# The second weight chunk in halves between those of the first, and conversion passes moved behind the first steps' copies

## The chip, the cores and the metric

One core of one Trainium2 chip runs the whole program. The metric is the device time of one execution in microseconds; the kernel before was measured in four runs. A core has five engines that work at once, each through its own queue in order: PE (TensorE, the matrix multiplier, which writes to PSUM), DVE (VectorE), ACT (ScalarE), POOL (GpSimd) and SP (SyncE, which here only issues DMA transfers). Engines wait for each other through semaphores.

## The reference, cut to what matters

```python
batch, seq, dim = (8, 3008, 256)
X = np.fft.fft(x, axis=1)
X = np.fft.fft(X, axis=2)
x = X.real.astype(np.float32).reshape(B * S, D)
h = x @ w_in                                # w_in:  256 x 2048
g = h * (1.0 / (1.0 + np.exp(-1.702 * h)))
return (g @ w_out).astype(np.float32)       # w_out: 2048 x 256
```

A two-dimensional Fourier transform of eight sequences, of which the real part is kept, and on it two matrix products with a quick GELU between them. Both weight matrices arrive in double precision.

## The kernel before, in words

**The transform.** The sequence length is split as 3008 = 47 x 64. `mix_first` (and `mix1` for later sequences) does the 47-point part as matmuls, the result goes through DRAM (`spill_first`, `fill`), and `stage2` does the 64-point part for one block of four groups; its result is transposed by DVE into the tile `pq`. The transform over the 256 columns is not done on the data: it is folded into `w_in`. `fold_w(n)` multiplies chunk n of `w_in` (512 columns) by a cosine and sine table and leaves the product in `wcs`. It needs eight matmuls of 512 columns, four for each half i of the rows (i = 0 and i = 1), which add up in two PSUM banks; ACT copies both out (line 474).

**The weights' conversion.** A chunk is 512 columns of `w_in` (in0 to in3) or 512 rows of `w_out` (out0 to out3), 1024 doubles per partition, loaded as pairs of 32-bit words (`load_in`, `load_out`, on SP's queue, into a ring of three buffers `raw`). It becomes float32 in steps on three engines:

| step | engine, line | what it needs |
|---|---|---|
| `squares` | ACT 401 | the raw chunk |
| `clamp` | POOL 406 | the raw chunk |
| `low_up`, `low_down` | ACT 411, 416 | the raw chunk, each other |
| `high` | DVE 433, 434, 435 | squares, clamp |
| `finish_in`, `finish_out` | POOL 447, 455 | high, low_down |

`prepare` takes the buffers for it. `bounds` is prepare, squares, clamp, low_up and low_down at once, `finish` is one of the finishing steps. `finish_in` writes `wst`, which fold_w reads; `finish_out` writes `wo`, which the output products read.

**The steps.** The work on the data is a list of 384 steps t: 8 sequences, 3 blocks, 2 halves, 8 pairs of 128 hidden features. In the first eight steps (t < 8) a step is: `hidden(t)` (PE: sixteen matmul records into the banks `pa` and `pb`; ACT copies pa to `v`, line 515), `rows(t)` (DVE lines 553, 556, 544: it reads v, pb, `nb`, pa and gives both halves of the hidden values), `activate(t)` (ACT line 562) and `product(t)` (PE, into the output banks, three steps later: LAG = 3). `nyquist(0, 0)` makes `nb` through PE and an ACT copy (line 372), `first_row(n)` makes `af` for chunk n (PE `psf`, ACT lines 482 and 483), `rotate` corrects one column (PE `psr`). `warm` is a matmul whose result nobody reads. Steps from 8 on run another, larger loop body that the change leaves alone.

**What sets the order.** The schedule is written out by hand: instructions go to each engine's queue in the order of the calls. Before the loop stands a list of calls (lines 874 to 908). In the loop, `extra` holds what is appended to the end of a step, by `at(t, fn, ...)`; fold_w(2) and fold_w(3) stand in steps 3 and 5 (`early`). PSUM banks for the opening come in turn from a ring of six names, and each call of `bank` moves on by one; from step 5 on the ring is cut, and step 5 asks for two banks by name:

```python
    spare = ["b0", "b1", "b2", "o2", "o3", "o4"]
...
        pa, pb = (bank(name, f"b{i}" if t == NP - 3 else None) for i, name in enumerate(("pa", "pb")))
```

Of the kernel before, what the change touches and what calls it, by code (L numbers as in the profile page):

```python
# [111 lines left out]
def kernel(ctx: ExitStack, tc, x, w_in, w_out, tab1, tab2, out):  # L112
    nc = tc.nc
# [53 lines left out]
    def bank(name, tag=None):  # L167
        if tag is None:
            tag = spare.pop(0)
            spare.append(tag)  # L170
        if tag in ("o0", "o1"):
            return o_banks[int(tag[1])]
        return (rest if tag[0] == "o" else psp).tile([128, 512], F32, tag=tag, name=name)
# [5 lines left out]
    def halves(out, lhs, rhs, **how):  # L179

        for c0 in (0, 64):
            nc.tensor.matmul(out[c0:c0 + 64], lhsT=lhs[:, c0:c0 + 64], rhs=rhs, skip_group_check=True, **how)  # L182
# [137 lines left out]
    def warm(n):  # L320

        ps = bank("warm")
        for _ in range(n):
            nc.tensor.matmul(ps[:], lhsT=wcs[0][:, 0:128], rhs=wcs[0][:, 0:512], start=True, stop=True)
# [11 lines left out]
    def rotate(b, a0=0, a1=NG, copy=None):  # L336

        col = t4t[b][:, a0:a1, H]
        ps = bank("psr")
        halves(ps[:, 0:a1 - a0], rot, col, start=True, stop=True)  # L340
        (copy or nc.vector.tensor_copy)(col, ps[:, 0:a1 - a0])
# [39 lines left out]
    def load_in(n, eng):  # L381
        t = raw["in", n] = ring("raw").bitcast(U32).rearrange("p (n w) -> p n w", w=2)
        eng.dma_start(out=t[:].rearrange("p (i f) w -> p i (f w)", i=2),
                      in_=w_in[:, n * 512:(n + 1) * 512].bitcast(U32).rearrange("(i p) f -> p i f", p=128))
# [8 lines left out]
    def prepare(key):  # L393


        pre[key] = ring("s"), ring("m"), ring("r").bitcast(U32)

    def squares(key, eng):
        g, hi = pre[key][0], raw[key][:, :, 1].bitcast(F32)
        if eng is nc.scalar:  # L400
            eng.activation(g[:], hi, ACTF.Square)
        else:
            eng.tensor_tensor(g[:], hi, hi, op=ALU.mult)

    def clamp(key, lo=0, n=1024):
        nc.gpsimd.tensor_scalar(pre[key][1][:, lo:lo + n], raw[key][:, lo:lo + n, 1].bitcast(F32), scalar1=TOP, scalar2=-TOP,
                                op0=ALU.min, op1=ALU.max)

    def low_up(key, lo=0, n=1024):

        nc.scalar.activation(pre[key][2][:, lo:lo + n].bitcast(F32), raw[key][:, lo:lo + n, 0], ACTF.Copy, scale=2.0 ** -29,
                             bias=2.0 ** 23)

    def low_down(key, lo=0, n=1024):
        r = pre[key][2][:, lo:lo + n]
        nc.scalar.activation(r, r.bitcast(F32), ACTF.Copy, bias=-2.0 ** 23)
# [8 lines left out]
    def high(key, lo=0, n=1024):  # L425

        g, m, _ = (t[:, lo:lo + n] for t in pre[key])
        bits = m.bitcast(U32)
        if lo == 0:
            made_a[key] = ring("a").bitcast(U32)  # L430
        a = made_a[key][:, lo:lo + n]
        dve = nc.vector
        dve.scalar_tensor_tensor(m, g, LOW * LOW, m, op0=ALU.is_ge, op1=ALU.mult)
        dve.tensor_scalar(a, bits, scalar1=3, scalar2=0x3FFFFFF8, op0=ALU.logical_shift_left, op1=ALU.bitwise_and)
        dve.scalar_tensor_tensor(a, bits, 0xC0000000, a, op0=ALU.bitwise_and, op1=ALU.bitwise_or)
# [5 lines left out]
    def finish_in(n, lo=0, k=1024):  # L441

        if lo == 0:
            wst[n] = op.tile([128, 2, 512], F32, tag="os", name="wst")
        key, part = ("in", n), slice(lo, lo + k)
        out = wst[n][:].rearrange("p i f -> p (i f)")[:, part]
        nc.gpsimd.tensor_tensor(out.bitcast(U32), made_a[key][:, part], pre[key][2][:, part], op=ALU.add)
# [16 lines left out]
        for out, i0, i1 in ((t1, b12, b11), (t2, b22, t1), (t3, b22, b12), (t4, b21, t2)):  # L464
            nc.gpsimd.tensor_tensor(out, i0, i1, op=ALU.subtract)

    def fold_w(n):
        ps = [bank("psw") for _ in range(2)]
        for i in range(2):
            for cs in range(2):  # L470
                halves(ps[cs][:], cd[:, i, cs, :], wst[n][:, i, :], start=(i == 0), stop=(i == 1))
        for cs in range(2):

            nc.scalar.copy(wcs[cs][:, n * 512:(n + 1) * 512].rearrange("p (f c) -> p f c", f=4),
                           free(ps[cs][:], 0, [1, 4], [4, 128]))
# [379 lines left out]
    for i, need in enumerate(((0, 7), (1,), (6,), (2,), (5,), (3,), (4,), ())):  # L855
# [8 lines left out]
        if i in (4, 5):  # L864
            h0 = 512 * (i - 4)
# [12 lines left out]
        spill_first(k, 16, NM, (nc.sync, nc.sync))  # L878
    prepare(in1)
    squares(in1, nc.scalar)  # L880
    for h0 in (0, 512):
        finish_in(0, h0, 512)
    clamp(in1)
    low_up(in1)
    low_down(in1)
    high(in1)
    load_out(1, nc.sync)
    fill(0, 4, NG)
    warm(1)
    fold_w(0)  # L890
    warm(1)
    first_row(0)
    prepare(out0)
    finish_in(1)
    clamp(out0)
    rotate(0, 0, 4, nc.scalar.copy)
    squares(out0, nc.scalar)
    stage2(0, 0)
    warm(1)
    low_up(out0)  # L900
    low_down(out0)
    high(out0)
    load_in(3, nc.sync)
    prepare(in2)
    squares(in2, nc.scalar)
    clamp(in2)
    fold_w(1)
    finish_out(0)

    extra, early = {}, {}  # L910

# [1 line left out]
        extra.setdefault(t, []).append((fn, args))  # L913

    n = len(steps)

    for t, key in (1, in2), (2, ("out", 1)), (3, ("in", 3)), (5, ("out", 2)), (6, ("out", 3)):
        at(t, high, key)
        if key != in2:
# [1 line left out]
        at(t + 1, finish, key)  # L921
    early[3], early[5] = 2, 3
    rows_at = {1: 1, 4: 2, 6: 3}
    for t, c in ((0, 2), (1, 3)):
        at(t, load_out, c, nc.sync)
    at(3, load_matrices)
    if B > 1:
# [35 lines left out]
    for t in range(n + LAG):  # L963
        if t < NP:
            if t == NP - 3:
                spare[:] = [tag for tag in spare if tag[0] == "o"] + ["b2"]
            hidden(t)
            if t == NP - 1:
                middle(NP)
                begin(NP)  # L970
                nc.gpsimd.memset(wcs[1][0:1, :], 0.0)
            if t == 0:
                low_up(in2)
                nyquist(0, 0)
                low_down(in2)
            if t in rows_at:
                first_row(rows_at[t])
            if t >= LAG:
                product(t - LAG, 0, None)
            if t in early:  # L980
                fold_w(early[t])
            if t:
                activate(t - 1)
            rows(t)
            if t == NP - 1:
                doubled(NP)
                middle(NP + 1)
        else:
            after, special = (any(fn in (mix1, stage2) for fn, _ in extra.get(k, ())) for k in (t - 1, t))
            if t < n:  # L990
                begin(t, 1)
            if t == NP:
                activate(t - 1)
            if t < n:
                forward(t)
            if after and t + 1 < n:
                middle(t + 1)
            opening = (t - LAG) % NP == 0 and t >= NP + LAG
            one, other = (t - LAG, (1, 2, 4, 7)), (t - LAG - 1, (5, 6, 3))
            if opening:  # L1000
                small_products(*other)
            cut = 0 if opening and not after else 3 if after else 2
            product(t - LAG, 0, cut)
            if after:
                small_products(one[0], one[1][:1])
                small_products(other[0], () if opening else other[1][:1])
            if t + 1 < n:
                begin(t + 1)
            if not opening:
                small_products(other[0], other[1][after:])  # L1010
            product(t - LAG, cut, 6 if t - LAG == last else None)
            small_products(one[0], one[1][after:])
            swap(t - LAG - 2)
            if t < n:
                backward(t)
            if t + 1 < n:
                doubled(t + 1)
            if t < n:
                activate_back(t)
                sums(t, nc.gpsimd)  # L1020
            if t + 2 < n and not special:
                middle(t + 2)
            combine_small(t - LAG - 1)
            if t - LAG == last:
                product(last, 6, None)
            sums(t - 1, nc.vector)
            deeper(t - 2, 0)
            deeper(t - 3, 1)
        if t == NP:
            psu.close()  # L1030
            low = ctx.enter_context(tc.tile_pool(name="low", bufs=1, space=PS))
            pot["low"] = low.tile([128, 3 * 512], F32, tag="low", name="low")
        if t >= LAG:
            combine(t - LAG)
            combine_last(t - LAG - 2)
            turn_last(t - LAG - 3, 0)
            turn_last(t - LAG - 4, 1)
        if t >= NP:
            spare[:] = [f"b{t % 2}"] * special + ["b2"]
        for fn, args in extra.get(t, ()):  # L1040
            fn(*args)
# [28 lines left out]
```

## Time and profile before

| | |
|---|---|
| median of 4 runs | 1875.7 us (1869.67 to 1876.27) |
| the profiled execution's own time | 1875.91 us |
| its span (first to last instruction) | 1874.1 us |
| PE busy | 1847.7 us, 99% |
| DVE busy | 1531.1 us, 82% |
| ACT busy | 1150.7 us, 61% |
| POOL busy | 965.9 us, 52% |

All times in the timelines are from the start of the span. The stretch that the change touches goes from about 25 us, when PE has done `mix_first`, to about 80 us, when step 7 runs. In that stretch, by windows: PE is busy 12.60 of 15 us in 25 to 40, 10.00 of 10 in 40 to 50, 8.67 of 10 in 50 to 60 and 15.00 of 15 in 60 to 75; ACT is busy 9.06 of 10 in 40 to 50, and DVE 9.79 of 10 in 50 to 60. A row of a timeline gives start, length, engine, line, operation, output and input tiles, shape and count; in brackets the engine's idle time before it, and what released it. A matmul of float32 shows as two records, so "x8" are four matmuls. Line numbers are those of the kernel before.

### The profile page before, as it was taken

The numbers are of one execution on the slowest core, as the hardware profiler recorded it, in microseconds if no ns is written. First come the engines' busy times: TensorE is split into PE (matmuls) and PEld (weight loads), VectorE is DVE, ScalarE is ACT, GpSimd is POOL, SyncE is SP. The second block draws the span as 40 slices with busy tenths as digits, with TensorE's granted clock in tenths as the row PEclk, the third lists the DMA queues.
The fourth block names the chain that finished last, engine by engine and source line by source line (L and its number), as shares of the span: only waits on it lengthen the run. The fifth ranks groups of instructions, "written<-read, shape, count | busy, mean of one in ns | idle before, by whom it ended". The sixth has DMA issues, their size and how long they took to land.

```text
span 1874.1 us, 55830 instructions
## 1 busy us (share of the span) xinstructions
PE 1847.7 (99%) x23684; PEld 1421.2 (76%) x23684; DVE 1531.1 (82%) x2245; ACT 1150.7 (61%) x2248; POOL 965.9 (52%) x1058
## 2 busy tenths in 40 slices
PE   8999999999999999999999999999999999999998
PEld 5667777778777777777777778776877777778776
DVE  7788888888789877997789878887788888878874
ACT  6655665666556556666666666655566666656663
POOL 5577345744367443773347633475345754444442
PEclk9999999999999999999999999999999999999999
DMA  8720350125110350114402252122411021100111
GB/s 278 177 51 17 80 95 17 48 63 100 32 51 14 74 101 19 51 21 106 67 13 59 44 104 39 21 56 57 96 30 25 19 62 35 29 18 16 20 22 23
DMA packets 145686, 105.28 MB, mean 56 GB/s; under 512 B 105161, under 2 KB 128233, under 8 KB 144254
## 3 DMA queue, kind: packets, MB, share of 16 engines
q1 hardware_dynamic: 144222, 101.19, 24.9%
q8 instruction: 187, 3.06, 0.7%
q10 hardware_dynamic: 1216, 0.52, 0.1%
q14 instruction: 61, 0.50, 0.1%
HBM read 64.41 MB, written 48.05 MB: 60 GB/s over the span
## 4 chain that ended last, share of the span: by engine, by line
PE 88%; DVE 6%; ACT 3%; issue 1%; DMA 1%; POOL 0%; SPq 0%; DVEq 0%; ACTq 0%; POOLq 0%
PE x L182 32%; PE o L182 25%; PE low L664 23%; PE o L664 4%; DVE big L630 2%; PE ps L354 1%; PE ps L253 1%; DVE big L544 1%; DVE big L767 1%; ACT x L571 1%; DMA big<-in_moe_w_in_dram 1%; ACT xt L256 0%; ACT big L586 0%; ACT g L583 0%; DVE big L676 0%
## 5 line engine op out<-in xcount | busy, mean ns | idle before, releaser
L601 POOL TENSOR_TENSOR big<-big 128x256 f32<-128x256 f32 (+1 forms) x376 | 351.3, 934 | 846.1 <-ACT big L593 731.7
L182 PE MATMUL x<-pq,wcs 128*64 128x256 f32 (+1 forms) x6016 | 775.8, 378 | 6.1 <-ACT x L571 3.0
L630 DVE TENSOR_TENSOR big<-big 128x512 f32<-128x512 f32 (+1 forms) x736 | 639.2, 883 | 35.4 <-PE low L664 18.9
L182 PE MATMUL o<-big,wo 128*64 128x256 f32 (+1 forms) x4800 | 625.2, 376 | 2.0 <-DVE big L608 2.0
L182 PEld LDWEIGHTS x<-pq,wcs 128*64 128x64 f32 x6016 | 419.0, 137 | 190.4 <-ACT x L571 15.0
L182 PEld LDWEIGHTS o<-big,wo 128*64 128x64 f32 x4800 | 349.0, 137 | 143.6 <-DVE big L608 2.9
L583 ACT ACTIVATE g<-x 128x512 f32<-128x512 f32 (+1 forms) x376 | 222.0, 590 | 374.5 <-PE x L182 373.4
L544 DVE TENSOR_TENSOR big<-g,x 128x512 f32<-128x512 f32 (+2 forms) x440 | 253.8, 588 | 198.8 <-ACT big L586 198.3
L664 PE MATMUL low<-big 128*64 128x128 f32 (+1 forms) x5888 | 383.7, 270 | 4.0 <-issue 4.0
L664 PEld LDWEIGHTS low<-big 128*64 128x64 f32 x5888 | 338.8, 137 | 32.2 <-issue 4.3
L571 ACT ACTIVATE x<-nb,af 128x256 f32<-128x256 f32 (+1 forms) x752 | 352.7, 469 | 12.3
L602 POOL TENSOR_TENSOR big<-big 128x256 f32<-128x256 f32 (+1 forms) x376 | 358.9, 955 | 0.0
L586 ACT ACTIVATE big<-x 128x512 f32<-128x512 f32 (+1 forms) x376 | 220.5, 586 | 200.6 <-PE x L182 191.1
L593 ACT ACTIVATE big<-big 128x512 f32<-128x512 f32 (+1 forms) x376 | 231.8, 617 | 48.1 <-DVE big L544 46.0
L664 PE MATMUL low<-big,wo 128*64 128x128 f32 (+1 forms) x2944 | 222.4, 271 | 0.3 <-issue 0.2
L664 PEld LDWEIGHTS low<-big,wo 128*64 128x64 f32 x2944 | 173.8, 137 | 4.0 <-issue 0.4
L609 DVE TENSOR_TENSOR big<-big 128x512 f32<-128x512 f32 (+1 forms) x188 | 149.5, 795 | 6.5
L608 DVE TENSOR_TENSOR big<-big 128x512 f32<-128x512 f32 (+1 forms) x188 | 137.3, 731 | 4.8 <-POOL big L601 4.8
L767 DVE TENSOR_TENSOR big<-big,low 128x512 f32<-128x512 f32 (+3 forms) x184 | 109.1, 610 | 3.9 <-PE low L664 0.4
L664 PEld LDWEIGHTS o<-big,wo 128*64 128x64 f32 x1472 | 93.4, 137 | 23.9
L664 PE MATMUL o<-big,wo 128*64 128x128 f32 (+1 forms) x1472 | 110.7, 270 | 0.0
L225 POOL TENSOR_TENSOR xt<-xt 111x510 f32<-111x510 f32 x56 | 76.2, 1360 | 4.4
(103 smaller groups left out, 972.7 us busy)
## 6 DMA issues: line engine op xcount, KB each, us to landing
out_dram<-os SPq DMA_DIRECT2D x284, 64.0 KB
t<-Td SPq DMA_DIRECT2D x22, 512.0 KB
Td<-xt SPq DMA_DIRECT2D x14, 768.0 KB
xt<-in_x_dram SPq DMA_DIRECT2D x14, 512.0 KB
xt<-Xr SPq DMA_DIRECT2D x14, 512.0 KB
nb<-Nd SPq DMA_DIRECT2D x23, 256.0 KB
out_dram<-os SPq DMA_DIRECT2D x96, 56.0 KB
Xr<-in_x_dram SPq DMA_DIRECT2D x7, 752.0 KB
```

The costliest lines, as they stand in the source:

```text
L182: nc.tensor.matmul(out[c0:c0 + 64], lhsT=lhs[:, c0:c0 + 64], rhs=rhs, skip_group_check=True, **how)
L544: nc.vector.tensor_tensor(free(out, at + m - 1, [by, 2], [RUN, blocks], [-1, m]), *ins, op=op)
L571: nc.scalar.activation(x[:, i * 256:i * 256 + n], nbt[b, blk][:, hh * 256:hh * 256 + n], ACTF.Copy, scale=af1[:, f:f + 1])
L583: nc.scalar.activation(two(g[:], n), two(xb[t][:], n), ACTF.Copy, scale=2.0)
L586: nc.scalar.activation(front(t), two(xb[t][:], width(t)), ACTF.Gelu_apprx_sigmoid)
L593: nc.scalar.activation(back(t), back(t), ACTF.Gelu_apprx_sigmoid)
L601: eng.tensor_tensor(right(t, S1, n), left(t, A21, n), right(t, A22, n), op=ALU.add)
L602: eng.tensor_tensor(left(t, S3, n), left(t, A11, n), left(t, A21, n), op=ALU.subtract)
L608: eng.tensor_tensor(s2, s1, a11, op=ALU.subtract)
L609: eng.tensor_tensor(s4, a12, s2, op=ALU.subtract)
L630: nc.vector.tensor_tensor(out, i0, i1, op=how)
L664: nc.tensor.matmul(o, lhsT=lhs, rhs=rhs, start=first_in, stop=(p == NP - 2), skip_group_check=True)
```

## The change

`fold_w` can now be called for one half of the rows at a time: it takes its two banks with the first half and copies out with the second. In the list before the loop, in1's `high` and `finish_in` are done in two halves of 512, its clamp is put between the two halves of in0's `finish_in`, and the matmuls of fold_w(1) stand in two parts, one before the first `stage2` and one behind it. first_row(0) comes after that. Two of the `warm` calls are gone. Out0's `low_up` and `low_down` are moved into steps 0 and 1, `finish_out(0)` to the end of step 1, in2's `squares` and `low_up` into step 1 and its `low_down` into step 2. `load_in(3)` and the loads of out2 and out3 stand later among the calls, in the same order on SP's queue.

```diff
-    def fold_w(n):
-        ps = [bank("psw") for _ in range(2)]
-        for i in range(2):
+    folded = {}
+
+    def fold_w(n, parts=(0, 1)):
+        if parts[0] == 0:
+            folded[n] = [bank("psw") for _ in range(2)]
+        ps = folded[n]
+        for i in parts:
             for cs in range(2):
                 halves(ps[cs][:], cd[:, i, cs, :], wst[n][:, i, :], start=(i == 0), stop=(i == 1))
+        if parts[-1] == 0:
+            return
...
     squares(in1, nc.scalar)
-    for h0 in (0, 512):
-        finish_in(0, h0, 512)
+    finish_in(0, 0, 512)
     clamp(in1)
+    finish_in(0, 512, 512)
     low_up(in1)
     low_down(in1)
-    high(in1)
+    for h0 in (0, 512):
+        high(in1, h0, 512)
     load_out(1, nc.sync)
     fill(0, 4, NG)
     warm(1)
     fold_w(0)
-    warm(1)
+    prepare(out0)
+    for h0 in (0, 512):
+        finish_in(1, h0, 512)
+    clamp(out0)
+    fold_w(1, (0,))
+    rotate(0, 0, 4, nc.scalar.copy)
+    stage2(0, 0)
+    squares(out0, nc.scalar)
+    fold_w(1, (1,))
     first_row(0)
-    prepare(out0)
-    finish_in(1)
-    clamp(out0)
-    rotate(0, 0, 4, nc.scalar.copy)
-    squares(out0, nc.scalar)
-    stage2(0, 0)
-    warm(1)
-    low_up(out0)
-    low_down(out0)
     high(out0)
-    load_in(3, nc.sync)
     prepare(in2)
-    squares(in2, nc.scalar)
     clamp(in2)
-    fold_w(1)
-    finish_out(0)
...
+    at(1, finish_out, 0)
...
-    for t, c in ((0, 2), (1, 3)):
+    for t, c in ((1, 2), (2, 3)):
         at(t, load_out, c, nc.sync)
...
             if t == 0:
-                low_up(in2)
                 nyquist(0, 0)
-                low_down(in2)
+                low_up(out0)
+                load_in(3, nc.sync)
+            if t == 1:
+                low_down(out0)
             if t in rows_at:
                 first_row(rows_at[t])
+            if t == 1:
+                squares(in2, nc.scalar)
+                low_up(in2)
+            if t == 2:
+                low_down(in2)
```

## The prediction, made before the changed kernel ran

> **What bounds the kernel now.** I read the page first (busy shares, slices), then PE's waits, then the timelines of the four engines for 25 to 80 us, where all that the diff touches runs.
>
> ```profile
> PE 1847.7 (99%) x23684; PEld 1421.2 (76%) x23684; DVE 1531.1 (82%) x2245; ACT 1150.7 (61%) x2248; POOL 965.9 (52%) x1058
> ```
>
> TensorE (PE) is busy for 99% of the span: the main loop is bound by it, and the steps after the opening only move with the moment when the opening hands over. So the question is when PE gets through the opening. PE's timeline there (start, length, engine, line, tile, count, idle before and its releaser):
>
> ```profile
> 26.91 1.94 PE L182 MATMUL psw<-wst,small 128*64 128x512 f32 x8 [0.96 <-POOL wst L447]
> 29.34 1.94 PE L182 MATMUL psw<-wst,small 128*64 128x512 f32 x8 [0.49 <-POOL wst L447]
> ...
> 36.20 3.65 PE L182 MATMUL psw<-wst,small 128*64 128x512 f32 x16 [0.95 <-POOL wst L447]
> 39.68 1.03 PE L182 MATMUL pa<-pq,wcs 128*64 128x256 f32 x8
> ...
> 52.74 3.65 PE L182 MATMUL psw<-wst,small 128*64 128x512 f32 x16 [0.62 <-POOL wst L447]
> ...
> 58.88 0.63 PE L182 MATMUL psf<-twos,wcs 1*64 1x1 f32 x16 [0.71 <-DVE big L544]
> ...
> 63.03 1.06 PE L182 MATMUL pa<-pq,wcs 128*64 128x256 f32 x8
> ```
>
> PE waits for the converted weights (`wst`, written by POOL) of chunks 0, 1 and 2, and once for DVE's `rows(3)`. The first step's `pa` starts at 39.68, step 5's at 63.03 without a wait. From 39.68 on PE idles only 1.33 us up to 75 us: an earlier start could be kept only if the other engines kept up.
>
> ACT's timeline, the first steps:
>
> ```profile
> 41.25 1.17 ACT L411 ACTIVATE big<-big 128x1024 f32<-128x1024 uint32 x1
> 42.63 0.59 ACT L372 COPY nb<-psn 128x512 f32<-128x512 f32 x1 [0.22 <-PE psn L182]
> 43.11 1.06 ACT L416 ACTIVATE big<-big 128x1024 uint32<-128x1024 f32 x1
> ...
> 49.39 0.56 ACT L515 COPY v<-pa 128x512 f32<-128x512 f32 x1
> ```
>
> L411 and L416 are chunk in2's `low_up` and `low_down`, done by 44.2; step 2's `v` copy comes at 49.39, behind out1's three passes. DVE's and POOL's timelines, where they get in each other's way:
>
> ```profile
> 23.98 0.43 DVE L434 TENSOR_SCALAR big<-big 128x512 uint32<-128x512 uint32 x1
> 25.76 1.38 DVE L434 TENSOR_SCALAR big<-big 128x512 uint32<-128x512 uint32 x1
> ...
> 52.17 1.61 DVE L433 SCALAR_TENSOR_TENSOR big<-big 128x1024 f32<-128x1024 f32 x1
> 53.88 1.49 DVE L434 TENSOR_SCALAR big<-big 128x1024 uint32<-128x1024 uint32 x1
> ...
> 63.83 0.69 DVE L544 TENSOR_TENSOR big<-pa,dif 128x512 f32<-128x512 f32 x1
> ...
> 50.32 2.37 POOL L447 TENSOR_TENSOR wst<-big 128x1024 uint32<-128x1024 uint32 x1 [4.91 <-DVE big L435]
> 52.67 2.15 POOL L406 TENSOR_SCALAR big<-big 128x1024 f32<-128x1024 f32 x1
> ```
>
> The same L434 takes 0.43 with POOL idle and 1.38 with POOL busy. L433 (1.22 elsewhere) starts at 52.17 but seems to run only once POOL's L447 ends at 52.69; POOL's L406 (1.12 elsewhere) then runs only after L433, and L434 after L406. They take turns.
>
> [...]
>
> **The change, part by part.** The instructions are the same but for two warm-up matmuls fewer, three more on DVE and one on POOL (`high` and `finish_in` of in1 in two pieces); the rest is order.
>
> 1. *Chunk 1 in halves between those of chunk 0.* Removed from PE: two `warm`, 1.0 each, and the 0.95 wait at 36.20. But POOL and DVE, which ran in1's `clamp`, `high` and `finish_in` one after another from 29.25 to 36.14, now interleave, and lock each other out. Step by step: POOL's first in0 half ends at 26.86; L434 holds the lock to 27.14; the moved clamp of in1 (1.12) takes it to 28.26; in0's last L435 (0.69), at 27.18 before, ends at 28.95 in place of 27.87. DVE goes straight on with in1's first L433 (0.68) to 29.6, so in0's second `finish_in` runs 29.6 to 30.85 (1.25), against an end of 29.29. L434 waits for it: 31.3; L435 32.0; next L433 32.65; in1's first `finish_in` 33.9; L434 34.35; L435 35.05; the second half 35.15 to 36.4. On PE, with 1.74 for four 512-wide matmuls (half of 36.20 to 39.68): chunk 0's second half 30.9 to 32.65, chunk 1's first 33.95 to 35.7, `psr` 0.2 and `stage2` 1.1 to 37.0, chunk 1's second half 38.75, `psf` 0.56: step 0 starts at T = 39.3, against 39.68. All that was removed buys 0.4 us. Without any lock wait the same sum gives T = 36.6. Those are the two ends; I take 39.3, because the trace shows the lock.
>
> 2. *ACT's queue.* Now behind the first steps' copies are out0's `low_up` and `low_down` and all three passes of in2, which before ran at 35.8 to 39.0 or right after 41.25. The `nb` copy starts at T+2.95, as before. From there, start to start by the rows of before: nb 0.48, low_up(out0) 1.15, v(1) 0.49, low_down(out0) 0.97, af 0.12, squares(in2) 1.06, low_up(in2) 1.15, activate(0) 0.95, out1's three 1.06, 1.22 and 0.97: 9.62, so v(2) starts at T+12.57 = 51.9, against 49.39. Behind it low_down(in2): 0.46 and 1.06 more, ended at T+14.1 = 53.4, against 44.2. POOL's `finish_in(2)` waits for it now, not for DVE: 53.5 to 55.85 (2.37). Chunk 2's fold starts on PE at 55.9, against 52.74: +3.15. PE, through with `product(0)` at about 52.9, idles some 3 us.
>
> 3. *DVE behind finish_in(2).* rows(2) ends near 54.6; out1's L433 then finds POOL in finish_in(2) until 55.85. Before, that release was at 52.69. From it the same chain follows (out1's `high`, rows(3), in3's `high`, rows(4)), which ended at 64.52; now 3.15 later, at 67.7.
>
> 4. *Banks.* Two fewer `warm` turn the ring of PSUM banks by two: step 4 now takes b0 and b1, which step 5 asks for by name. So step 5's `pa` must wait for rows(4), where before it waited for nobody. Before, it would have lost 64.52 - 63.03 = 1.5; now it starts at 67.7, against 63.03: +4.65. PE gets there at 66.2, after a wait of 0.85 for rows(3).
>
> 5. *Moved at no cost.* `finish_out(0)` goes to step 1: POOL gets to it after low_down(out0), near 45.5, and it collides with in2's `high` to about 49; product(0) needs it then, and waits for activate(0) at about 48.7 anyway. If DVE fell behind there, rows(2) would be late, but it waits for v(2) until 52.45. SP's queue keeps its order: in3's load, released by low_up(out0) at about 43.4 in place of 42.10, is needed at 54 and landed at 51.6 with out2's load beside it, which now starts 5 us later; out2, out3, the tables and the x loads all go out 1.5 to 5 us later, and their users are tens of us away (`fold1` at 108.97).
>
> From step 5 on the order is the old one and each engine hangs on PE's (`fold_w(3)`, ACT's 6.31 us wait for it, v(6), rows(6), `pb` of step 7), so the 4.65 stays. The profiled execution, 1875.91 with a span of 1874.1, would become 1880.6; from the median of 1875.7 (0.2 below it), **1880.4 us**, +0.25%. About 0.3% (5.6 us) is what a measurement of this kernel can tell from no change.
>
> **The rivals.**
> - *The lock costs little in the halves* (T = 36.6, or arbitration kinder than I take it). Then finish_in(2) ends near 53.2, +0.5, and step 5 waits for rows(4): +2.0, 1877.7. For it: only L433 and L434 are seen blocked in the trace, L435 never. [...]
> - *The early start is kept.* If ACT has more room than I count, PE gains 36.6 - 39.68 = -3.1, 1872.6. It decides where finish_in(2) ends by about 49.6 and rows(4) by 60, 6 and 8 us before my times; the count of ACT's passes speaks against it.
> - *Slower beyond doubt: PE's clock falls.* [...] By the start of the trace half rate lasts 5.6 us, that is 2.8 us of work lost; 2.35 of it vanish in the two waits that follow, unless these also grow because v(4) is late. If the clock stays low longer, or the gap at 32.65 counts as well, +2.5: 1882.9. [...] against it: gaps of 2.2 us leave the rate alone.
> - *The change does not start step 0 earlier* is the first part of my forecast already.
>
> **How the numbers follow.** Forecast 0.52, lock cheap 0.24, early start kept 0.08, clock or another wait on top 0.16. Slower by over 0.3%: most of the last case and some 0.2 of the first, whose sum stands only 1 us short of the bound: 0.14 + 0.12 + 0.01 for a chance drift, with a little for terms that I left out, 0.33. Faster by over 0.3%: PE's idle and warm-up time from 25 to 80 us is 4.5 + 2 us in all, so nearly all of it would have to go: 0.03. Within: 0.64. The range takes the cheap lock and half of the last rival, and 2 to 3 us of drift (one of the four runs shown is 6 us below the rest): 1874.5 to 1884.5. The likeliest case alone is 1878.5 to 1882.
>
> **What would show it.** In the profile of the changed kernel: step 0's first `pa` at 39.3 (36.6 if the lock is cheap); L434 and L435 of in1 at over 1 us each; v(2) near 51.9; in2's L416 after v(2) and L447 for in2 released by ACT L416, not DVE; PE's wait before chunk 2's fold about 3 us; step 5's `pa` released by DVE L544 near 67.7. The prediction is wrong if chunk 2's fold starts before 54 or step 5's `pa` finds its bank free; and if warm matmuls are seen at half rate after 56 us, the clock rival holds.

## The result and the profile after

The changed kernel takes 1877.09 us (median of 43 runs, 1871.49 to 1880.8) against 1873.77 us (64 runs, 1868.23 to 1878.65) for the kernel before. The ratio of the two on record is 1.0020 [1.0013, 1.0026], or 3.7 us more (the two medians are 3.3 apart). Forecast were 0.25% more and, as the likeliest verdict, a difference within 0.3%.

The profiled execution of the changed kernel took 1874.97 us, with a span of 1873.2. That is 0.9 us *less* than the profiled execution of before, so the spans alone would mislead. The loss has to be sought in the stretch that was changed. PE's timeline of the changed kernel there (start, length, engine, line, operation, tiles, shape, count; idle time before and its releaser):

```profile
26.75 1.94 PE L182 MATMUL psw<-wst,small 128*64 128x512 f32 x8 [0.69 <-POOL wst L447]
30.34 1.94 PE L182 MATMUL psw<-wst,small 128*64 128x512 f32 x8 [1.66 <-POOL wst L447]
33.08 1.94 PE L182 MATMUL psw<-wst,small 128*64 128x512 f32 x8 [0.81 <-POOL wst L447]
...
38.52 1.08 PE L182 MATMUL pa<-pq,wcs 128*64 128x256 f32 x8
...
55.04 5.28 PE L182 MATMUL psw<-wst,small 128*64 128x512 f32 x16 [3.38 <-POOL wst L447]
...
66.88 1.08 PE L182 MATMUL pa<-pq,wcs 128*64 128x256 f32 x8 [0.54 <-DVE t L341]
...
83.31 1.08 PE L182 MATMUL pb<-pq,wcs 128*64 128x256 f32 x8 [0.81 <-DVE big L550]
```

Step 0's `pa` starts at 38.52, 1.16 us sooner than before (39.68). Chunk 2's fold starts at 55.04, 2.30 later than before (52.74), behind a gap of 3.38, and takes 5.28 in place of 3.65. Step 5's `pa` starts at 66.88, 3.85 later than before (63.03). From there the distance stays. Step 7's `pb` is 3.86 later, by the line above and this one of the kernel before:

```profile
79.45 1.08 PE L182 MATMUL pb<-pq,wcs 128*64 128x256 f32 x8 [0.81 <-DVE big L544]
```

Lines past `fold_w` have moved by six (L515 is now L521, L544 is L550). The releaser "DVE t L341" is inferred. The copy of `t` stands right behind rows(4), whose L550 ended at 66.73, in DVE's queue. ACT's timeline of the changed kernel shows the moved passes:

```profile
42.01 1.19 ACT L411 ACTIVATE big<-big 128x1024 f32<-128x1024 uint32 x1
...
45.70 1.20 ACT L411 ACTIVATE big<-big 128x1024 f32<-128x1024 uint32 x1
...
50.96 0.57 ACT L521 COPY v<-pa 128x512 f32<-128x512 f32 x1
51.43 1.06 ACT L416 ACTIVATE big<-big 128x1024 uint32<-128x1024 f32 x1
```

The first L411 is out0's. The second is in2's `low_up`, and in2's `low_down` (L416) starts at 51.43, behind v(2); before, it started at 43.11. POOL's timeline has the consequence, and the collisions in the opening; DVE's is below it:

```profile
26.66 1.36 POOL L406 TENSOR_SCALAR big<-big 128x1024 f32<-128x1024 f32 x1
28.71 1.57 POOL L447 TENSOR_TENSOR wst<-big 128x512 uint32<-128x512 uint32 x1 [0.70 <-DVE big L435]
...
44.70 3.58 POOL L455 TENSOR_TENSOR wo<-big 128x512 uint32<-128x512 uint32 x2 [4.95 <-ACT big L416]
...
52.62 2.37 POOL L447 TENSOR_TENSOR wst<-big 128x1024 uint32<-128x1024 uint32 x1 [3.22 <-ACT big L416]
```

```profile
27.01 1.55 DVE L435 SCALAR_TENSOR_TENSOR big<-big 128x512 uint32<-128x512 uint32 x1
...
29.20 1.37 DVE L434 TENSOR_SCALAR big<-big 128x512 uint32<-128x512 uint32 x1
30.60 0.69 DVE L435 SCALAR_TENSOR_TENSOR big<-big 128x512 uint32<-128x512 uint32 x1
...
48.32 1.63 DVE L434 TENSOR_SCALAR big<-big 128x1024 uint32<-128x1024 uint32 x1 [1.17 <-POOL wo L455]
...
53.68 2.39 DVE L433 SCALAR_TENSOR_TENSOR big<-big 128x1024 f32<-128x1024 f32 x1
```

`finish_in(2)` waited 3.22 us and was released by ACT's L416, no longer by DVE. At 27.01 an L435, which takes 0.69 alone, took 1.55 beside POOL's clamp (L406); L434 (0.43 alone) took 1.37 beside POOL's L447; and L433 (1.22 alone) took 2.39 beside `finish_in(2)`. In these rows each of DVE's three conversion lines is held up by POOL.

The busy times by windows of the changed kernel (PE, PEld, DVE, ACT, POOL, with counts; then the granted PE clock) have one more thing:

```profile
50.00:60.00 10.00, 6.62 (x32) 2.43 (x28) 9.47 (x11) 7.63 (x9) 5.48 (x3) 0.83 0.99 312
```

The clock was 0.83 in 50 to 60 (1.00 before), and 0.50 in each of the three us from 55 to 58. That is 1.7 of 10 us of full speed lost, and the fold took 1.63 longer. Whether the gap of 3.38 is the cause is tested below.

### The profile page after: what moved, and what is told of

Read it like the earlier page. It is cut to its first block, busy times and chain, and to the rows that moved or that the text cites. A ratio compares the mean times of both kernels' runs of the same rounds, so it can differ in the third digit from the quotient of the medians.

```text
span 1873.2 us, 55828 instructions
## 1 busy us (share of the span) xinstructions
PE 1846.3 (99%) x23680; PEld 1416.5 (76%) x23680; DVE 1531.8 (82%) x2248; ACT 1150.5 (61%) x2248; POOL 967.0 (52%) x1059
## 4 chain that ended last, share of the span: by engine, by line
PE 88%; DVE 6%; ACT 4%; issue 1%; DMA 1%; POOL 0%; SPq 0%; ACTq 0%; DVEq 0%; POOLq 0%
PE x L182 32%; PE o L182 24%; PE low L670 23%; PE o L670 4%; DVE big L636 2%; PE ps L354 1%; PE ps L253 1%; DVE big L773 1%; DVE big L550 1%; ACT x L577 1%; PE ps L306 1%; ACT xt L256 0%; ACT big L592 0%; DVE big L682 0%; PE psw L182 0%
## 5 line engine op out<-in xcount | busy, mean ns | idle before, releaser
L550 DVE TENSOR_TENSOR big<-g,x 128x512 f32<-128x512 f32 (+2 forms) x440 | 253.8, 588 | 203.7 <-ACT big L592 203.3
```

The source lines that it names most:

```text
L550: nc.vector.tensor_tensor(free(out, at + m - 1, [by, 2], [RUN, blocks], [-1, m]), *ins, op=op)
```

## The experiments

The theory was that of the prediction, with times taken from the trace: in2's late `low_down` moves chunk 2's fold, and the turned ring of banks makes step 5 wait for rows(4). The rivals: the halves themselves cost time, or the fallen clock does. Landmarks are counted here from the start of fold_w(0), which stands ahead of everything that the change touches, since from one profiled execution to another the whole opening shifts by some tenths of a us. The expectations, written earlier, count from the start of the span, from step 0 or from the last warm-up matmul after the mixing (fold_w(0) starts 1.39 to 3.01 behind that).

```
kernel            step 0  fold of chunk 2          step 5   step 7  median us (runs)  ratio to before
                    pa    start  gap   length        pa       pb
before            12.77   25.83  0.62   3.65       36.12    52.54   1873.77 (64)      1
after             11.77   28.29  3.38   5.28       40.13    56.56   1877.09 (43)      1.0020 [1.0013, 1.0026]
after_again       11.77   28.25  3.37   5.35       40.08    56.54   1877.87 (22)      1.0019 [1.0009, 1.0030]
banks_alone       12.79   25.85  0.63   3.65       37.89    54.32   1875.84 (12)      1.0008 [0.9997, 1.0020]
passes_alone      12.78   29.24  3.38   3.65       39.59    56.02   1874.62 (12)      1.0007 [0.9995, 1.0020]
halves_alone      11.76   26.91  0.62   3.65       37.25    53.67   1872.94 (12)      0.9995 [0.9982, 1.0009]
after_banks_back  11.76   28.29  3.40   6.39       40.53    56.95   1877.92 (18)      1.0019 [1.0007, 1.0030]
after_warm        11.76   28.28  0.64   3.65       40.20    56.63   1874.78 (20)      1.0009 [1.0000, 1.0017]
after_warm_banks  11.76   28.27  0.60   3.65       38.56    54.98   1872.06 (12)      0.9992 [0.9983, 1.0001]
warm_banks_again  11.76   28.32  0.66   3.65       38.54    54.95   1872.21 (22)      0.9991 [0.9982, 0.9999]
after_in2_sooner  11.76   27.00  1.04   3.65       39.30    55.72   1877.37 (10)      1.0024 [1.0011, 1.0037]
clamp_back        12.59   29.05  3.33   5.35       40.86    57.30   1879.07 (22)      1.0027 [1.0017, 1.0038]
combined          10.93   24.96  1.59   3.65       35.23    51.65   1873.84 (12)      0.9991 [0.9977, 1.0005]
combined_again    11.48   25.38  1.46   3.65       35.66    52.06   1872.72 (14)      0.9991 [0.9979, 1.0003]
```

Counted so, the starts in the two profiled executions of one kernel agree within 0.05 us, but for `combined` (0.41 to 0.55). Each ratio was taken against executions of the kernel before in the same set, so it is not the quotient of the medians shown; the kernel before had medians of 1872.32 us (51 executions), 1874.64 (39) and 1873.50 (67) in the three sets. The timed ratios are far coarser than the landmarks, so what follows rests on the landmarks, and the times only bound it.

**The banks alone.** The kernel before, with the ring set in step 4 to the order that it has there in the changed kernel:

```diff
+            if t == 4:
+                spare[:] = ["b0", "b1", "b2", "o2", "o3", "o4"]
             hidden(t)
```

> The kernel before, with nothing changed but the ring of banks at step 4, so that steps 4 and 5 both take b0 and b1, as in the changed kernel. Bank theory: step 5's first pa now waits for rows(4), which ended at 64.52, so it starts near 64.65 in place of 63.03, and step 7's pb at 81.0 in place of 79.45; the time grows by 1.5 us (0.08%). Rival, that the bank costs nothing because the fold of chunk 3 or step 7 waits for something else anyway: step 5's pa late, step 7's pb still at 79.45.

PE's timeline of this kernel:

```profile
64.93 1.08 PE L182 MATMUL pa<-pq,wcs 128*64 128x256 f32 x8 [2.38 <-DVE t L341]
```

Everything up to chunk 2's fold is as before, and step 5 is 1.77 later; the prediction had 1.5 for this case. The bank wait is real, and it appears with nothing else changed.

**The moved passes alone, the halves alone.** The first is the kernel before with ACT's passes, `finish_out(0)` and the loads moved as in the change. The second is the changed kernel with these put back and the ring of before:

```diff
     stage2(0, 0)
     warm(1)
-    low_up(out0)
-    low_down(out0)
     high(out0)
-    load_in(3, nc.sync)
     prepare(in2)
-    squares(in2, nc.scalar)
     clamp(in2)
     fold_w(1)
-    finish_out(0)
...
```

```diff
     fold_w(1, (1,))
     first_row(0)
+    low_up(out0)
+    low_down(out0)
     high(out0)
+    load_in(3, nc.sync)
     prepare(in2)
+    squares(in2, nc.scalar)
     clamp(in2)
+    finish_out(0)
+    spare[:] = spare[2:] + spare[:2]
...
```

> The kernel before (chunk 1 in one piece, both warm-up calls, its banks) with only the conversion passes moved as in the changed kernel: out0's low_up and low_down, finish_out(0) and all of in2's passes in steps 0 to 2. Queue theory: step 0 starts as before, near 39.7; v(2) comes some 2.5 us later than before and low_down(in2) behind it; chunk 2's fold starts 3.4 us later than before, behind an idle time of some 3 us, and step 7's pb 3.5 us later. This part alone then costs about what the whole change costs. Rival, that the halves or the banks make the loss: less than 1.5 us.

> The changed kernel with the passes put back ahead of the steps (out0's low_up and low_down, in2's squares and finish_out(0) before the loop, in2's low_up and low_down in step 0) and with the banks of the kernel before: only chunk 1's halves are left. Queue theory: step 0 starts 1.2 us earlier than before on PE, but ACT is still with out0 and in2 then, so that v(0) comes near 42, no earlier than before; chunk 2's fold starts within 1.5 us of the kernel before, on the late side, and step 7's pb 0 to 1.5 us later than before. Rival, that the early start of step 0 carries through: step 7's pb a good 1 us earlier than before.

The passes alone bring 3.41 at chunk 2's fold and 3.48 at step 7, nearly the whole loss. The halves alone start step 0 1.01 sooner and still lose 1.13 by step 7. ACT's timeline of `halves_alone` has the reason:

```profile
39.03 1.21 ACT L411 ACTIVATE big<-big 128x1024 f32<-128x1024 uint32 x1
...
43.84 0.57 ACT L372 COPY nb<-psn 128x512 f32<-128x512 f32 x1
```

Out0's passes, which ran at 35.79 before, stand behind the copies of chunk 1's fold and of first_row(0) here, and step 0's `nb` copy stands behind them: 16.81 from fold_w(0), against 15.72 before. So an early step 0 needs the passes out of its way. With the passes moved too (`after_warm_banks`, step 7 at 54.98) the halves gain 1.04 against `passes_alone`, at full clock in both (1.00 in 50 to 60) and with the banks of before. The two parts of the change fit each other; only the sum is still behind.

**The banks in the changed kernel, and the clock.** One run turns the ring back by two, one fills the gap before chunk 2's fold with one more `warm` call of three matmuls, whose results nobody reads, and one does both. The line behind `warm(3)` gives its bank back to the ring:

```diff
     n = len(steps)
+    spare[:] = spare[2:] + spare[:2]      # after_banks_back, after_warm_banks
     at(1, finish_out, 0)
...
+            if t == 3:                    # after_warm, after_warm_banks
+                warm(3)
+                spare.insert(0, spare.pop())
             if t in early:
                 fold_w(early[t])
```

> The changed kernel with the ring of banks turned on by two before the loop, so that all steps have the banks of the kernel before. Bank theory: step 5's pa no longer waits for rows(4) (66.73); PE is through with psr at 66.34, so it starts near 66.35 in place of 66.88 and step 7's pb near 82.8 in place of 83.31. So of the 3.86 us of the whole change the banks would be worth 0.5 as long as chunk 2's fold is late, not the 1.5 that they cost alone. Rival, that the late fold is not what holds PE: step 5's pa near 64.7.

> The changed kernel with three warm-up matmuls put into PE's idle time ahead of chunk 2's fold (step 3), and the banks otherwise as in it. The fold there took 5.28 us in place of 3.65. Clock theory: it ran at half rate after 3.38 us of idling, and with the gap filled it takes 3.65 again. Whether that mattered: by my sum step 5's pa waits for rows(4) at 66.73 in any case, so it stays at 66.88 and step 7's pb at 83.3, with a wait for rows(3) near 61 in between. Rival, that the slow fold is 1.6 of the 3.86 us: step 7's pb at 81.7.

> The changed kernel with PE's idle time ahead of chunk 2's fold filled by three warm-up matmuls and with the banks of the kernel before. With the clock up and the bank free, PE waits only for rows(3) near 61.0 and goes on to step 5's pa at 65.3, 1.6 us earlier than in the changed kernel; step 7's pb near 81.8, 2.3 us later than in the kernel before. Bank theory: of the 3.9 us, 1.6 are the banks', once the clock does not hide them. Rival, that rows(4) is needed at once anyway by step 5's own rows: no gain over the changed kernel.

PE's timelines of the three, in this order:

```profile
55.51 6.39 PE L182 MATMUL psw<-wst,small 128*64 128x512 f32 x16 [3.40 <-POOL wst L447]
```

```profile
56.13 3.65 PE L182 MATMUL psw<-wst,small 128*64 128x512 f32 x16 [0.64 <-POOL wst L447]
...
68.05 1.08 PE L182 MATMUL pa<-pq,wcs 128*64 128x256 f32 x8 [1.51 <-DVE t L341]
```

```profile
55.53 3.65 PE L182 MATMUL psw<-wst,small 128*64 128x512 f32 x16 [0.60 <-POOL wst L447]
...
65.82 1.06 PE L182 MATMUL pa<-pq,wcs 128*64 128x256 f32 x8
```

The first was a miss: with the bank free, step 7 came 0.39 later and not sooner, because the fold took 6.39 at the fallen clock (0.71 in 50 to 60), and PE itself was late for step 5. How long the fold takes behind such a gap differs between executions (5.28 to 6.39 where the clock fell). With the 5.28 of the changed kernel, the free bank would have been worth the 0.54 of the wait seen there. With the clock kept up (1.00 in 50 to 60) but the bank taken, step 7 is where it was (56.63 against 56.56): PE waits 1.51 for rows(4) in place of 0.54. With both mended it is 1.58 sooner. So the fallen clock and the bank wait hide each other. Mending the clock alone moved nothing at step 7, mending the bank alone is worth 0.5 at most, and both together 1.58.

**in2's low_down sooner.** In step 1, right behind in2's `low_up`, in place of step 2:

```diff
                 low_up(in2)
-            if t == 2:
                 low_down(in2)
```

> The changed kernel with in2's low_down put right behind its low_up in step 1, so that ACT does it ahead of out1's three passes and of step 2's v. Queue theory: low_down(in2) ends near 48 in place of 52.5, finish_in(2) then starts when DVE's high of in2 is done (51.2) and ends at 53.7 in place of 54.99; chunk 2's fold starts at 53.8 in place of 55.04, with an idle time of 2.1 us or less; activate(0) comes 1 us later. Step 5's pa near 66.0, step 7's pb near 82.4 in place of 83.31. Rival, that DVE and POOL's locking sets the end and not ACT's queue: chunk 2's fold within 0.3 of 55.04 and step 7's pb unmoved.

POOL's timeline of this kernel:

```profile
52.80 2.36 POOL L447 TENSOR_TENSOR wst<-big 128x1024 uint32<-128x1024 uint32 x1 [1.98 <-DVE big L435]
```

Chunk 2's fold comes 1.29 sooner than in the changed kernel, as expected, and step 7 0.84; step 5 still waits 1.49 for its bank. The releaser of `finish_in(2)` is DVE's L435 again, so what remains of the fold's lateness, 1.17, comes by DVE. Its in2 `high` ran into `finish_out(0)` on POOL, which this row of DVE's timeline shows:

```profile
49.76 1.60 DVE L434 TENSOR_SCALAR big<-big 128x1024 uint32<-128x1024 uint32 x1 [1.17 <-POOL wo L455]
```

**The place of in1's clamp.** Behind both halves of in0's `finish_in`, as it was before the change:

```diff
     finish_in(0, 0, 512)
-    clamp(in1)
     finish_in(0, 512, 512)
+    clamp(in1)
```

> The changed kernel with in1's clamp back behind both halves of in0's finish_in, as in the kernel before. Lock theory: POOL then no longer holds up in0's last L435 (1.55 us long in the changed kernel, 0.69 again here), chunk 0's second half starts 1.3 us earlier on PE, but in1's high starts that much later; chunk 1's first half and step 0 come about 0.5 us later than in the changed kernel, and so does all that hangs on ACT's queue: from the first warm-up call behind the first mixing to step 7's pb 58.8 us, against 58.3. Rival, that the lock costs more than the interleaving brings: step 0 earlier than in the changed kernel.

Step 0 comes 0.82 later and step 7 0.74. In spite of the delay that it causes (1.55 in place of 0.69 for one L435), the clamp between the halves is the better place.

**A combination.** From the parts that paid: conversion of in1 in halves on DVE and POOL, but its fold in one piece; out0's passes ahead of step 0; in2's `squares` and `low_up` around `nb` in step 0 and its `low_down` in step 1; in3's bounds in step 3; the loads of out2 and out3 in steps 0 and 1 again; the banks of before.

```diff
-    fold_w(1, (0,))
     rotate(0, 0, 4, nc.scalar.copy)
     stage2(0, 0)
     squares(out0, nc.scalar)
-    fold_w(1, (1,))
+    low_up(out0)
+    low_down(out0)
     first_row(0)
     high(out0)
+    load_in(3, nc.sync)
     prepare(in2)
     clamp(in2)
+    fold_w(1)
+    spare[:] = spare[2:] + spare[:2]
...
             if t == 0:
+                squares(in2, nc.scalar)
                 nyquist(0, 0)
-                low_up(out0)
-                load_in(3, nc.sync)
+                low_up(in2)
+            if t == 3:
+                bounds(("in", 3))
...
             if t:
                 activate(t - 1)
+            if t == 1:
+                low_down(in2)
             rows(t)
```

> What the runs so far point to: chunk 1 made in halves by DVE and POOL, but folded in one piece behind the first stage2; the banks of the kernel before; out0's passes before step 0, in2's squares and low_up around step 0's nb copy and its low_down in step 1; in3's passes in step 3 in place of the end of step 2, since in3's load lands only at 51.6. By the durations seen so far step 0 starts 1.5 us earlier than in the kernel before, chunk 2's fold 1.3 us earlier, and step 7's pb 0.5 to 1.0 us earlier, which the time can hardly tell (0.05%). Rival, that the lock between DVE and POOL takes all of it: step 7's pb no earlier than in the kernel before.

Step 7 comes 0.89 and, in the second set, 0.48 sooner than before, and chunk 2's fold 0.87 and 0.45 where 1.3 was expected. Here the landmark matters. fold_w(0) itself started 3.01 and 1.39 behind the last warm-up matmul in these two executions (1.98 before). In both, POOL's `wst` released PE there, after a wait of 1.99 and 0.36 (0.96 before). That in0's load landed later or earlier is the author's estimate of the reason and was not shown. Counted from that matmul, step 7 comes 0.14 later in the first and 1.07 sooner in the second. The times say 0.9991 twice, with intervals that reach over 1. So that the combination is ahead of the kernel before is likely, but not shown.

**Repeats.** The changed kernel, `after_warm_banks` and `combined` once more, in a set with `clamp_back`:

> The changed kernel once more, in the same call as the next two, so that they are compared on one chip. By the traces the opening is 3.8 us longer than before: ratio 1.0020.

> The changed kernel with the filled gap and the banks of the kernel before, once more. In its trace the opening is 2.2 us longer than in the kernel before, which asks for a ratio of 1.0012; in its first times it was 0.9992 (0.9983 to 1.0001). If the opening is all that differs, the ratio comes out near 1.0012 and below that of the changed kernel by 0.0008. Rival, that half a clock after the gap costs more in most executions than in the two profiled ones, or that something behind the opening is faster: near 0.9992 again.

> The combined kernel once more. In its trace the opening from chunk 0's fold on is 0.9 us shorter than in the kernel before: ratio 0.9995. Its first times gave 0.9991 (0.9977 to 1.0005). It is the faster of all where it stays at or below 0.9995 with an interval that leaves out 1.

The landmarks came again. The times did not follow them: `warm_banks_again` was expected near 1.0012 and came at 0.9991, where its rival had it, and `combined_again` has 0.9991 with an interval that does not leave out 1. The kernels with the filled gap time lower than their openings say. `after_warm` has the opening of the changed kernel and a ratio of 1.0009 in place of 1.0019 or 1.0020. Step 7 of `after_warm_banks` is 2.4 behind before, yet it takes 1.5 and 1.7 us less in the two sets (0.08% and 0.09% of 1873.77; the first interval reaches over 1). The lists of times show how. The highest of `warm_banks_again` is 1874.61 and that of before in the same set 1881.14; the lowest are 1869.62 and 1868.18, a difference of 1.4 that has the sign of the opening's. These kernels lack the long executions.

What makes an execution long is in the waits of PE, of `after_banks_back`, whose profiled execution (1880.99) was the longest of its 18, and of before:

```profile
PE low L670 <- issue: 3.8, 1, 3.8
```

```profile
PE low L664 <- issue: 4.2, 2, 4.0
```

(columns: us in total, times, longest.) "issue" is time in which PE waited for nothing that the profile shows. The changed kernel's profiled execution had 2.4 of it in all, `clamp_back`'s and `warm_banks_again`'s none. All pauses of 1.9 us or more end at one place of the program, 1309 to 1315 us from the start of the span. Behind the longest of them the clock was low, as in this window of before:

```profile
1310.00:1320.00 10.00, 10.00 (x102) 8.83 (x100) 4.42 (x8) 3.73 (x8) 1.42 (x2) 0.73 0.20 54
```

With 0.93 in the ten us ahead of it, that is 3.4 us of full speed lost, beside a pause of 4.0. Over the 14 profiled executions, the time less step 7's start from the start of the span goes from 1788.3 and 1788.5 (no such pauses) to 1796.8 and 1796.5 (3.8 and 4.2 us of them), with a correlation of 0.95. The pauses alone make half of this range. With the clock's loss from 1300 to 1330 us taken off too, 1788.3 to 1790.1 is left, so after step 7 all these kernels run alike within 1.8 us but for the pauses and the low clock behind them. This is why the profiled span after is shorter than before in spite of an opening 3.86 longer: it takes 4.8 us less from step 7 on, with 1.8 less of pauses and 3.4 less of lost clock there.

The mean granted clock, which is on record for each execution, points the same way. None of the 54 executions of the kernels with the filled gap is below 0.998. Of the 157 of the kernel before in the three sets, 52 are at 0.997, and these average 1876.0 to 1876.8 us by set, against 1870.8 to 1872.3 at 0.999. The changed kernel averages 0.9972 and `after_warm` 0.9989. As an estimate, 0.0017 of 1875 us is 3.2 us, more than the 1.63 that the profiled fold lost. So a rival has something for it, that the gap costs more by the clock in unprofiled executions than in the profiled ones. The lists don't say where in an execution the clock was low, so this is not shown. Why the kernels with the filled gap lack the long executions of the kernel before stays open.

## Why the prediction was right

The forecast of 0.25% more (measured 0.20%, 0.13 to 0.26) came out in the opening by the mechanism that it gave, with each landmark forecast some 0.8 us too late. Counted from fold_w(0), the opening lost 4.02 us. That the whole time came so near is in part luck. `after_warm` loses as much in its opening and takes only 0.09% more, so a part of the 3.7 us may go by the clock, which the forecast had among the rivals.

1. *Chunk 1 in halves.* Predicted T = 39.3, measured 38.52. This is the term that was mis-sized. The turns that DVE and POOL take, which the forecast calls the lock, are there, and all three of DVE's conversion lines show them (L435 1.55 in place of 0.69, L434 1.37 in place of 0.43, L433 2.39 in place of 1.22), but most hand-overs were 0.1 to 0.2 shorter than the sum had it: in these rows a held-up instruction took as long as if it ran from some 0.14 before the end of the other's record. The rest, 0.2, is that this execution's opening started sooner. So in0's second `finish_in` ended at 30.28 in place of 30.85, in1's first half at 33.03 in place of 33.9. The rival "the lock costs little" (36.6) is ruled out by the trace, and step 0 started 1.2 us sooner than before in place of the 0.4 of the forecast. The overlap of 0.14 is in L433's 2.39 beside the 2.37 of POOL's L447 too: it was 1.31 from L433's start to the end of L447, and 1.31 and the 1.22 that it takes alone make 2.53.
2. *ACT's queue.* The count of passes held: from step 0 to v(2) 12.44, predicted 12.57. `finish_in(2)` was released by L416 as predicted, at 52.62 (53.5). Chunk 2's fold came 2.30 later in place of 3.15, and 0.8 of that difference is the error in T. `passes_alone` shows that the moved passes, with `finish_out(0)`, make this lateness with nothing else changed, and `after_in2_sooner` that 1.29 of it hang on `low_down`'s place in ACT's queue.
3. *DVE behind finish_in(2).* rows(4) ended at 66.73 (67.7), for the most part again by the error in T.
4. *Banks.* Step 5's `pa` waited for rows(4) at 66.88 (67.7): +3.85 in place of +4.65. `banks_alone` gave 1.77 where 1.5 was predicted. What the step did not say is that the fallen clock can take the place of the bank wait: `after_banks_back`, with the bank free and a fold of 6.39, was no faster.
5. *Moved at no cost.* `finish_out(0)` collided with in2's `high` as described (3.58 in place of 2.51; L434 delayed to 48.32), and DVE was still through 0.35 before v(2). In the changed kernel it cost nothing; once `low_down` is sooner it is the next bound (`after_in2_sooner`).

The rival of the falling clock came true in part: the fold took 5.28. At the landmarks its price did not come on top, since rows(4) was later anyway: `after_warm`, at full clock, has the same step 7 to 0.07 us. In the times it may have come on top, as said above. The length of gap from which the clock falls was not shown by the trace of before. Its gaps of 2.20 and 2.03 us, before 107.9 and 113.99, stand at a clock of 1.00. The forecast overlooked its pause of 4.0 us at 1309, with the clock at 0.73 in the ten us from 1310 on. The half rate of 5.6 us is read from the start of that trace, where the weight loads of the warm-up matmuls are 0.85 us apart from 3.64 to 7.91 and 0.43 from 8.46 on; the profile's clock reads 1.00 there as well, so that this is the same slowing was the author's estimate. "The early start is kept" fell with step 2: step 0 came 1.00 us sooner and chunk 2's fold 2.46 later (both from fold_w(0)). The parts don't add: 3.48 (passes), 1.78 (banks) and 1.13 (halves) make 6.39 alone and 4.02 together, because the halves change sign: they cost 1.13 with the passes ahead of the steps and gain 1.04 with the passes behind them. One upon the other, passes +3.48, halves -1.04, banks +1.65 (`after_warm` less `after_warm_banks`) and the unfilled gap -0.07 make the 4.02.

## What to carry to other kernels

A start made sooner is worth only what the in-order queues behind it can follow (here ACT's, where in2's L416 ran at 51.43, behind v(2), in place of 43.11): before passes are put behind copies, count the queue to the instruction that the next stage waits for. A bank ring that goes on with each call couples places far apart; when calls are taken out, look up who gets which bank by name. Two waits that end close together hide each other, so mend them together or expect little from either.

## What was unexpected of the hardware

- PE's clock fell in four of five profiled executions with a gap of 3.33 to 3.40 us (folds of 5.28, 5.35, 5.35 and 6.39), but not in `passes_alone` behind 3.38 (3.65). Gaps of nearly one length had different effects, from 0 to 2.74 us more for the fold; what decides between them was not shown. Even the gap of 2.2 us before 107.9, which left the clock alone in the profile of before (1.00 from 105 to 115), was followed by a fall in others (0.69 in 110 to 115 us in `combined`, where the eight records after it took 1.72 in place of 0.98). It cost nothing there: PE's wait for DVE that follows shrank from 2.03 to 0.34.
- PE pauses of up to 4.0 us, for which the profile shows no wait, come and go between executions of one program, the long ones all at one place (1309 to 1315 us). The two longest, 3.8 and 4.0, were followed by 3.4 us of lost clock each. Among the profiled executions, the pauses and this loss explain all but 1.8 of a range of 8.5 us, which is larger than the effect of this change.
- DVE's L435 is held up by POOL like L433 and L434 (1.55 in place of 0.69); the trace of before had only shown the other two.
